# Two sweeps over d_ff and products from three float32r parts in an mLSTM cell with a feed-forward block

## The chip, the core and the metric

The kernel runs on one core of a Trainium2 chip. Its engines are TensorE (PE in the profile, with its weight loads shown apart as PEld), VectorE (DVE), ScalarE (ACT), GpSimd (POOL) and SyncE (SP), which here only issues DMAs. The metric is the device time of one execution in microseconds, median of several runs; smaller is better. All data are float32, apart from the weights, which lie in HBM as float64 and are read as 64-bit words (`U64`).

## The reference

An mLSTM cell runs over 4 batches, 8 heads, 768 tokens and head size 40; its output, 3072 tokens by 320, goes through a feed-forward block with d_ff = 2048:

```python
for t in range(S):                                   # per batch and head
    m_new = max(f_gate[t] + m, i_gate[t])
    C = exp(f_gate[t] + m - m_new) * C + exp(i_gate[t] - m_new) * outer(v[t], k[t])
    n = exp(f_gate[t] + m - m_new) * n + exp(i_gate[t] - m_new) * k[t]
    y[t] = sigmoid(o_gate[t]) * (C @ q[t]) / max(|n . q[t]|, 1)
x = y as (3072 tokens, 320)
h = x @ w_in                                         # 320 -> 2048
out = max(0.01 * h, h) @ w_out                       # 2048 -> 320
```

## The kernel before

**The cells.** The 768 tokens of a batch are cut into 6 chunks of 128; a step `s` is one chunk of one batch, with its 8 heads, and there are 24 steps, four to a chunk (`s = 4c + b`). Inside a chunk the recurrence is written as small matmuls with a decay mask: `u_parts` multiplies keys with queries (L598) and states with keys (L603), DVE applies the mask (L608) and adds to the state (L580), `u_mix` multiplies with the values and the state (L679), and DVE, POOL and DVE again turn that into x (L686, L617 to L619, L690, L693, L697). `gates` makes the decays of a chunk; they go to HBM (`a_dr`) and come back spread over the partitions (L397, L405).

**How a step's data comes.** Nearly all DMAs are issued by SP, in one order that the scheduler fixed when the program was built: k (L340), v in four pieces (L343), the decays (L397, L405), and k, q and the output gate in blocks, four DMAs each (L382). From chunk 2 on x goes out to HBM in four DMAs for a step (L700) and comes back transposed to `xT` in four more (L714). The steps use four rotating sets of buffers for k, v and the decays and two for the blocks (`rb`), so loads run two to four steps ahead.

**The weights** are loaded as 64-bit words (L213, L218) and made float32 by `narrow_weights`: one ACT and six DVE instructions per piece (L231 to L247). Both matrices are then held in SBUF whole.

**The feed-forward** runs per chunk, 512 tokens at a time (`ff_units`). First layer: the 320 inputs are cut in five slices of 64 rows; for each of the 16 blocks of 128 outputs five matmuls, 64 rows by 128 outputs by 512 tokens (for the first chunk 256), add up in PSUM. Two blocks go side by side, one on array rows 0 to 63, the other on rows 64 to 127 (`rows`, L743). ACT applies the leaky ReLU from PSUM to `acts` (L751). Second layer: for each of four groups of 128 tokens, 16 matmuls, 128 by 128 by 320 (`part`, L778), then an ACT copy and a DMA to the output (L786, L787). An f32 matmul appears in the trace as two weight loads and two matmuls, so L743 has 1120 instructions for 560 matmuls and L778 768 for 384.

**Order of the work.** PE, DVE, ACT and POOL run in the order in which the Python code emits it. `first_chunk` does chunk 0's cells. Then loop `c` = 1 to 6 emits the feed-forward of chunk c-1 as units (16 of first layer, 16 of second) and puts the cells of chunk c between them, at places written out by hand (`place`, `pairs`); in loop 6 there are no cells left. In loop 1 the remaining weights are narrowed, a few instructions per unit (`now`).

Of the kernel before, what the change touches and what calls it, by code (L numbers as in the profile page):

```python
# [9 lines left out]
F32 = mybir.dt.float32  # L10
U32 = mybir.dt.uint32
U64 = mybir.dt.uint64
AF = mybir.ActivationFunctionType
ALU = mybir.AluOpType
PSUM = bass.MemoryType.PSUM


@with_exitstack
def kernel(
# [51 lines left out]
    assert KR == DP and KC == 5 and KC * DP == Dm and GT * 4 <= 2048  # L71

    consts = ctx.enter_context(tc.tile_pool(name="consts", bufs=1))
    gp = ctx.enter_context(tc.tile_pool(name="gates", bufs=1))
    wk = ctx.enter_context(tc.tile_pool(name="wk", bufs=2))
    psf = ctx.enter_context(tc.tile_pool(name="psf", bufs=4, space=PSUM))
    psc = ctx.enter_context(tc.tile_pool(name="psc", bufs=4, space=PSUM))
# [22 lines left out]
    ident = consts.tile([P, P], F32, name="ident")  # L100
# [24 lines left out]
    acts = consts.tile([P, NF, GT], F32, name="acts")  # L125
    acts_l = acts[:].rearrange("p f t -> p (f t)")
    for n in range(NL):
        nc.vector.memset(kn[:, n, :, D:], 0.0)
        nc.vector.memset(qn[:, n, :, D:], 0.0)
        nc.gpsimd.memset(S_t[n][:, 1, :, D:], 2.0)  # L130
        nc.gpsimd.memset(S_t[n][SL:, 0], 0.0)
# [30 lines left out]
    QN = NF // 4  # L162
    QC = 4 * P
    WC = KC * 2 * P
    w_in = consts.tile([P, QN, WC], F32, name="w_in")
    w_out = consts.tile([P, NF, Dm], F32, name="w_out")

# [3 lines left out]

    def w_row(r, slot, j):
        n, e = divmod(j, 2)
        at = (2 * slot + e) * P
        return w_in[DP * r : DP * (r + 1), n, at : at + P]
# [6 lines left out]
    HW = 2 * Dm  # L182
    wide = moe_w_in.dtype == U64
    raws = {}
    if wide:
        raw_t = consts.tile([P, 5 * HW], U64, name="raw")

    def load_weights(n):

        m = n - QN  # L190
        if n < QN:
            dst = w_in[:, n, :]
        else:
            dst = w_out[:, 2 * m : 2 * m + 2, :].rearrange("p a d -> p (a d)")
        to = dst
        if wide:
            if n < 2:
                at = NF * GT - 2 * WC * (n + 1)
                raw = acts_l[:, at : at + 2 * WC].bitcast(U64)
            elif n < QN:  # L200
                raw = raw_t[:, WC * (n - 2) : WC * (n - 1)]
            elif m < 2:
                raw = w_out[:].rearrange("p f d -> p (f d)")[:, (2 + m) * WC : (3 + m) * WC].bitcast(U64)
            else:
                at = (4, 0, 1, 2, 3, 4)[m - 2] * HW
                raw = raw_t[:, at : at + HW]
            raws[n] = (raw, dst)
            to = raw
        if n < QN:
            src = moe_w_in[:, n * QC : (n + 1) * QC].rearrange("(k p) (r c) -> r p k c", p=DP, r=2)  # L210
            for slot in range(KC):
                for r in range(2):
                    nc.sync.dma_start(  # L213
                        to[DP * r : DP * (r + 1), 2 * P * slot : 2 * P * (slot + 1)], src[r, :, SLOTS[r][slot], :],
                    )
        else:
            rows = moe_w_out[2 * m * P : 2 * (m + 1) * P, :]
            nc.sync.dma_start(to.rearrange("p (a d) -> p a d", d=Dm), rows.rearrange("(a p) d -> p a d", p=P))  # L218

    def narrow_weights(n):  # L220
# [3 lines left out]
        if not wide:  # L224
            return
        raw, dst = raws.pop(n)
# [20 lines left out]
        nc.vector.tensor_tensor(dst, dst, low, op=ALU.add)  # L247


    a_dr = dr.tile([NB, 2, 2, BH, SL], F32, name="a_dr")  # L250
    x_dr = dr.tile([NS, Dm, P], F32, name="x_dr")
    gT, gL = {}, {}
# [95 lines left out]
    def load_o(s):  # L348
        c, b = divmod(s, B)
        at = NF * GT - 4 * WC - (s + 1) * Dm  # L350
        st[s]["o"] = acts_l[:, at : at + Dm]
        nc.sync.dma_start(  # L352
            st[s]["o"].rearrange("p (h d) -> p h d", d=D), o_gate[b, :, ts(c, P), :].rearrange("h p d -> p h d"),
        )
# [35 lines left out]
    def spread(s):  # L390
# [3 lines left out]
        w = wk.tile([P, H, P], F32, name="w", bufs=NL)  # L394
        d["w"] = w[:].rearrange("p h t -> p (h t)")[:, : H * SL].rearrange("p (h t) -> p h t", t=SL)
# [13 lines left out]
    def spread_first(a, s2):  # L409


        ab = [psf.tile([P, 2, H // RG, P], F32, name=f"ab{r}", tag="mm") for r in range(RG)]
        for n in range(2):
            for m in range(H // RG):
                for r in range(RG):
# [5 lines left out]
                    )  # L421
        for n in range(2):
            w = st[s2 + n]["w"] = wk.tile([P, H, P], F32, name="w", bufs=NL)
# [42 lines left out]
    def prep_qs(s):  # L466
# [3 lines left out]
        d["qs"] = wk.tile([P, Dm], F32, name="y")[:].rearrange("p (h d) -> p h d", d=D)  # L470
# [232 lines left out]
    def gather_x(s):  # L703

        c, b = divmod(s, B)
        if ("xT", c) not in st:
            st["xT", c] = wk.tile([P, KC, GT], F32, name="xT", bufs=1)
        xT = st["xT", c]
        src = x_dr[s].rearrange("(k p) t -> p k t", p=DP)
        for r in range(2):  # L710
            at = 0
            while at < KC:
                k0, n = run_of(r, at)
                nc.sync.dma_start(xT[DP * r : DP * (r + 1), at : at + n, ts(b, P)], src[:, k0 : k0 + 2 * n - 1 : 2, :])  # L714
                at += n

    def u_x(s):
# [3 lines left out]
        if b == 0:  # L721
            st["xT", c] = wk.tile([P, KC, GT], F32, name="xT", bufs=1)
        xT = st["xT", c]
# [9 lines left out]
        nc.scalar.copy(xT[DP:, 2 * KF, tok], xt[:DP, KF, :])  # L733
        del st[s]


    def ff_units(g):
        xT = st["xT", g]

        def rows(j, ph, cols, slots):  # L740
            for slot in slots:
                for r in range(2):
                    nc.tensor.matmul(  # L743
                        ph[r][:, cols], lhsT=w_row(r, slot, j), rhs=xT[DP * r : DP * (r + 1), slot, cols],
                        start=(slot == 0), stop=(slot == KC - 1),
                    )

        def relu(j, ph, cols):
            for r in range(2):
                f = f_of(r, j)  # L750
                nc.scalar.activation(acts[:, f, cols], ph[r][:, cols], AF.Prelu, alpha=0.01)  # L751

        def pair(j):
            ph = []

            def first():
                ph.extend(psf.tile([P, GT], F32, name=f"ph{r}", tag="mm") for r in range(2))
                rows(j, ph, slice(0, GT), range(3))

            def second():  # L760
                rows(j, ph, slice(0, GT), range(3, KC))
                relu(j, ph, slice(0, GT))

            return [first, second]

        def half(j, h):
            ph = [psf.tile([P, GT], F32, name=f"ph{r}", tag="mm") for r in range(2)]
            cols = ts(h, GT // 2)
            rows(j, ph, cols, range(KC))
            relu(j, ph, cols)  # L770
# [3 lines left out]
        def part(n, m):  # L774
            if m == 0:
                po[n] = psf.tile([P, Dm], F32, name="po", tag="mm")
# [254 lines left out]
```

## Time and profile before

| what | us |
|---|---|
| median of the runs (3; 527.35 to 528.73) | 528.12 |
| span of the profiled execution, first to last instruction | 526.4 |
| PE, PEld busy | 513.2, 336.3 |
| DVE, ACT, POOL busy | 240.3, 168.1, 113.0 |
| L743 and L778, matmuls of the feed-forward, busy on PE | 215.2 and 211.1 |

The profile has no other time for the profiled execution than its span; the median of the timed runs is 1.7 us above it. The page gives busy time of each engine, then the span in 40 equal slices of 13.2 us, then the chain of work that ended last and the costliest groups. In a group's row stand line, engine, operation, tiles (out<-in), shapes, count, then busy time and the mean of one in ns, then the engine's idle time before them. Matmuls overlap, so their busy time is less than count times mean. SP is in none of the busy rows: issuing a DMA is shown only in SP's own timeline (`SPq`), where each row is one stretch of issues, with its start and length.

The stages, by start and end on PE: chunk 0's cells to about 50 us, loop 1 to 139.6, loops 2, 3 and 4 to 218.5, 297.2 and 376.0, loop 5 to 454.0, loop 6 to the end.

### The profile page before, as it was taken

The page shows a single profiled execution, that of the slowest core. Times are in us where ns is not written, and L with a number is a line of the kernel's source. Part 1 is how long each engine was busy: PE and PEld are TensorE (multiplying, and loading weights), DVE is VectorE, ACT ScalarE, POOL GpSimd, SP SyncE. Part 2 cuts the span into 40 slices and gives each one's busy share as a digit, 9 for nine tenths or more (in the row PEclk, how much of TensorE's full clock was granted, in tenths as well). Part 3 has the DMA queues.
Part 4 walks back from the last instruction along what each step waited for, and adds up shares of the span by engine and source line. Part 5 has one row for each costly group of instructions (what it writes and reads, how often), then busy time and mean ns, then how long its engine had stood idle before and what let it go on. Part 6 is the DMA issues. An engine that isn't in the chain of part 4 may idle for free.

```text
span 526.4 us, 11333 instructions
## 1 busy us (share of the span) xinstructions
PE 513.2 (97%) x4501; PEld 336.3 (64%) x4501; DVE 240.3 (46%) x431; ACT 168.1 (32%) x458; POOL 113.0 (21%) x145
## 2 busy tenths in 40 slices
PE   8889989999999999999999999999999999999997
PEld 7877878777555577555577555577554577544675
DVE  4679998999328446028445028344028230000000
ACT  4565865534534212034212124212125100122100
POOL 4244354152205121015021015021013010000000
PEclk9668999999999999999999999999999999999999
DMA  9977687888755626685626676626542112000000
GB/s 116 156 204 153 138 212 171 196 145 175 146 137 105 137 72 150 129 174 107 138 75 143 134 150 129 138 76 155 125 102 52 50 52 87 14 0 1 12 12 25
DMA packets 165284, 59.13 MB, mean 112 GB/s; under 512 B 128816, under 2 KB 156016, under 8 KB 165232
## 3 DMA queue, kind: packets, MB, share of 16 engines
q1 hardware_dynamic: 164848, 58.28, 51.0%
q8 instruction: 35, 0.57, 0.5%
q10 hardware_dynamic: 384, 0.13, 0.1%
q14 instruction: 17, 0.14, 0.1%
HBM read 51.68 MB, written 6.70 MB: 111 GB/s over the span
## 4 chain that ended last, share of the span: by engine, by line
PE 83%; SPq 6%; DVE 4%; DMA 2%; ACT 2%; issue 1%; POOL 1%; ACTq 0%; POOLq 0%
PE po L778 38%; PE ph L743 36%; PE pT L679 3%; SPq L213 3%; PE sd L598 3%; SPq L338 2%; SPq L352 1%; PE sd L603 1%; DMA rb<-in_q_dram 1%; DVE raw L245 1%; DVE qn L608 1%; DMA S<-in_v_dram 0%; DMA raw<-in_moe_w_in_dram 0%; PE tk L518 0%; PE hN L649 0%
## 5 line engine op out<-in xcount | busy, mean ns | idle before, releaser
L743 PE MATMUL ph<-xT,w_in 64*128 64x512 f32 (+1 forms) x1120 | 215.2, 536 | 0.6 <-ACT acts L751 0.6
L778 PE MATMUL po<-w_out,acts 128*128 128x320 f32 x768 | 211.1, 434 | 0.0
L778 PEld LDWEIGHTS po<-w_out,acts 128*128 128x128 f32 x768 | 144.5, 190 | 62.6 <-issue 4.1
L743 PEld LDWEIGHTS ph<-xT,w_in 64*128 64x128 f32 x1120 | 107.8, 189 | 94.4 <-issue 87.7
L751 ACT ACTIVATE acts<-ph 128x512 f32<-128x512 f32 (+1 forms) x112 | 53.9, 534 | 151.8 <-PE ph L743 151.7
L608 DVE TENSOR_TENSOR qn<-w,sd 64x512 f32<-64x512 f32 x40 | 27.4, 684 | 97.7 <-PE sd L603 57.1
L576 POOL TENSOR_TENSOR S<-S,f 40x336 f32<-40x336 f32 x36 | 30.9, 858 | 101.9 <-PE pT L679 65.8
L442 ACT ACTIVATE w<-w,gT 128x64 f32<-128x64 f32 (+1 forms) x192 | 51.1, 348 | 3.1 <-POOL w L434 2.1
L434 POOL TENSOR_TENSOR w<-w,i 128x512 f32<-128x512 f32 x20 | 28.1, 1411 | 104.7 <-ACT bu L294 53.0
L786 ACT COPY y<-po 128x320 f32<-128x320 f32 x12 | 5.1, 423 | 83.3 <-PE po L778 83.3
L786 ACT COPY hn<-po 128x320 f32<-128x320 f32 x12 | 5.1, 426 | 76.0 <-PE po L778 76.0
L686 DVE STREAM_TRANSPOSE hb<-pT 128x512 f32<-128x512 f32 x16 | 11.4, 714 | 39.2 <-PE pT L679 39.0
L495 DVE TENSOR_TENSOR qn<-kqT,ea 64x512 f32<-64x512 f32 x32 | 27.3, 854 | 0.9
L693 POOL TENSOR_TENSOR xb<-xb,den 128x320 f32<-128x320 f32 x16 | 11.7, 728 | 66.5 <-DVE xb L690 66.5
L598 PEld LDWEIGHTS sd<-kqT 40*64 40x64 f32 x640 | 19.9, 135 | 6.1 <-issue 6.1
L697 DVE STREAM_TRANSPOSE x<-xb 128x512 f32<-128x512 f32 x16 | 18.1, 1130 | 7.7 <-POOL xb L693 7.7
L598 PE MATMUL sd<-kqT 40*64 40x64 f32 x640 | 21.5, 220 | 0.0
L603 PE MATMUL sd<-S,vu 64*40 64x42 f32 x576 | 20.1, 214 | 0.7 <-POOL vu L462 0.7
L489 DVE STREAM_TRANSPOSE kqT<-rb 128x512 f32<-128x512 f32 x32 | 20.5, 677 | 0.0
L603 PEld LDWEIGHTS sd<-S,vu 64*40 64x40 f32 x576 | 18.6, 111 | 0.8 <-POOL vu L462 0.8
L580 DVE TENSOR_TENSOR S<-S,sd 40x336 f32<-40x336 f32 x36 | 18.1, 503 | 1.0
L679 PEld LDWEIGHTS pT<-qn,S 128*64 128x64 f32 x512 | 15.6, 138 | 3.6 <-issue 3.5
(126 smaller groups left out, 364.9 us busy)
## 6 DMA issues: line engine op xcount, KB each, us to landing
w<-a_dr SPq DMA_DIRECT2D x40, 128.0 KB
rb<-in_k_dram SPq DMA_DIRECT2D x64, 80.0 KB
rb<-in_q_dram SPq DMA_DIRECT2D x64, 80.0 KB
rb<-in_o_gate_dram SPq DMA_DIRECT2D x64, 80.0 KB
ea<-a_dr SPq DMA_DIRECT2D x32, 128.0 KB
kn<-in_k_dram SPq DMA_DIRECT2D x24, 160.0 KB
raw<-in_moe_w_out_dram SPq DMA_DIRECT2D x6, 640.0 KB
S<-in_v_dram SPq DMA_DIRECT2D x80, 40.0 KB
```

The source lines that it names most:

```text
L434: nc.gpsimd.tensor_tensor(w, w, cm2.unsqueeze(1).to_broadcast([P, H, SL]), op=ALU.add)
L442: yield nc.scalar.activation(w[:, h, :], w[:, h, :], AF.Exp, bias=gT[c][:, 0, bh : bh + 1], scale=1.0)
L489: nc.vector.transpose(d["kqT"][:, i].rearrange("p (h t n) -> p h n t", n=TS, t=QW), raw_blocks(s, i, QW).rearrange("p (h n) d -> p h n d", ...
L495: nc.vector.tensor_tensor(mixed(s)[rows, 1 - r], d["kqT"][rows, 1].rearrange("p (h t) -> p h t", t=SL), d["ea"][rows], op=ALU.mult,)
L576: nc.gpsimd.tensor_tensor(new, old, g, op=ALU.mult)
L598: nc.tensor.matmul(bank[1 - u][toks, h, :], lhsT=kqT[rows, 0, ts(h, SL)], rhs=kqT[rows, 1, ts(h, SL)], start=True, stop=True,)
L603: nc.tensor.matmul(dC[u][:, h].rearrange("p k d -> p (k d)"), lhsT=d["ku"][toks, h], rhs=S_v[s % NL][toks, u, h, :, :V1], start=True, stop ...
L608: nc.vector.tensor_tensor(mixed(s)[toks, u], w[toks], bank[1 - u][toks], op=ALU.mult)
L679: nc.tensor.matmul(pT[DP * r : DP * (r + 1), j * P + u * SL : j * P + (u + 1) * SL], lhsT=S[:, u, h, :], rhs=m[:, u, h, :], start=True, st ...
L743: nc.tensor.matmul(ph[r][:, cols], lhsT=w_row(r, slot, j), rhs=xT[DP * r : DP * (r + 1), slot, cols], start=(slot == 0), stop=(slot == KC ...
L751: nc.scalar.activation(acts[:, f, cols], ph[r][:, cols], AF.Prelu, alpha=0.01)
L778: nc.tensor.matmul(po[n][:], lhsT=acts[:, f, ts(n, P)], rhs=w_out[:, f, :], start=(f == 0), stop=(f == NF - 1),)
```

## The change

- **Two sweeps.** d_ff is cut in two halves. Sweep 1 is the old loop with half of the weights: per chunk 8 units of first layer and 8 of second, then the partial output goes to HBM (`y_dr`, L821). Sweep 2 comes after the last loop: 12 groups of 256 tokens, each with 4 units; x comes back from HBM (L745), the partial sum too (L1092), and the result is written (L1142). Because sweep 2 needs all x in HBM, the x of chunks 0 and 1, which earlier never left SBUF, are now written out too (`keep_x`, L757).
- **Three parts.** A float32 number is split into its high part and the rest: `h` is the number with the low 12 bits masked off; the parts are h, the rest (scaled by 4096 on the weight side), and a combination of both (`three`, `split_x`). Three float32r matmuls (L786) give two PSUM sums, from which one scaled addition makes the product (`joined`, L795 ACT and L796 DVE). Both layers of sweep 2 and the first of sweep 1 are done so; the second layer of sweep 1 (L815) stays f32. All float32r matmuls of the first layer have 256 columns, those of the second 320.
- **Splitting work.** x is split on DVE, ACT and POOL (L269 to L272), once per sweep; the weights of the first half's w_in in `first_chunk`, those of the second half in loop 6 and the first units of sweep 2 (`convert_b`: narrowing, then L240 to L248, for four pieces of 128 by 1280). In sweep 2 the activations are split too (`grow`: three DVE instructions and a POOL copy of 128 by 512 per unit, L1112 to L1115).
- **Memory.** The cells' buffers are closed before loop 6 and their room is taken by the second half's weights; sweep 1's buffers are closed before sweep 2. PSUM for the feed-forward goes from four banks of their own to two buffers of two banks.
- The places of the cells between the units are written anew (`place`, `pairs`), the exponentials are emitted four instead of three per unit. The matmuls of the cells, their DMAs and their buffers' numbers stay.

Counted on the built programs, SP issues 607 DMAs before the change and 755 after it; DVE has 433 and 720 instructions, ACT 468 and 592, POOL 150 and 241. The float32r matmuls are 1440 (sweep 1, first layer), 1440 (sweep 2, first layer) and 576 (sweep 2, second layer); 192 f32 matmuls of the second layer are left. The core of the diff:

```diff
+    def three(raw, w, parts, eng):
+        h = raw.bitcast(F32)[:, :WC]
+        nc.vector.tensor_scalar(h.bitcast(U32), w.bitcast(U32), scalar1=HIGH, scalar2=None, op0=ALU.bitwise_and)
+        yield
+        nc.scalar.copy(parts[0], h)
+        eng.tensor_tensor(w, w, h, op=ALU.subtract)
+        yield
+        yield
+        nc.scalar.activation(parts[1], w, AF.Copy, scale=SPLIT)
+        yield
+        eng.tensor_tensor(parts[2], parts[1].bitcast(F32), h, op=ALU.subtract)
+        yield
...
+    def split_x(x, h, parts, eng):
+        nc.vector.tensor_scalar(h.bitcast(U32), x.bitcast(U32), scalar1=HIGH, scalar2=None, op0=ALU.bitwise_and)
+        nc.scalar.copy(parts[0], h)
+        eng.tensor_tensor(parts[1], x, h, op=ALU.subtract)
+        nc.vector.scalar_tensor_tensor(parts[2], in0=h, scalar=JOIN, in1=x, op0=ALU.mult, op1=ALU.subtract)
...
+    def keep_x(s):
+        to = x_dr[s].rearrange("(k p) t -> p k t", p=DP)
+        at = 0
+        while at < KC:
+            k0, n = run_of(0, at)
+            nc.sync.dma_start(to[:, k0 : k0 + 2 * n - 1 : 2, :], xT[:DP, at : at + n, ts(s % B, P)])
+            at += n
...
+    def product(j, w, xs, cols):
+        q, e = divmod(j, 2)
+        ph = psf.tile([P, 2, 2, GH], F32, name="ph", tag="mm")
+        for v in range(3):
+            for slot in range(KC):
+                at = (2 * slot + e) * P
+                for r in range(2):
+                    rows = slice(DP * r, DP * (r + 1))
+                    nc.tensor.matmul(
+                        ph[:, r, v // 2, :], lhsT=w[v][rows, q, at : at + P], rhs=xs[v][rows, slot, cols],
+                        start=(slot == 0 and v != 1), stop=(slot == KC - 1 and v != 0),
+                    )
+        return ph
+
+    def joined(ph, pool, out):
+        e = pool.tile([P, 2, GH], F32, name="e", bufs=2)
+        nc.scalar.copy(e[:], ph[:, :, 1, :])
+        nc.vector.scalar_tensor_tensor(out, in0=ph[:, :, 0, :], scalar=JOIN, in1=e[:], op0=ALU.mult, op1=ALU.add)
...
+        def first(j, half):
+            cols = ts(half, GH)
+            ph = product(j, wi, late_tiles["xs"], cols)
+            f = f_of(0, j)
+            a = acts[:, f : f + 3 : 2, cols]
+            joined(ph, fp, a)
+            nc.scalar.activation(a, a, AF.Prelu, alpha=0.01)
...
-        place = (2, 5, 7, 10, 12, 15, 16, 18, 21, 22, 24, 26, 28)
+        place = (1, 2, 3, 5, 6, 7, 8, 9, 10, 11, 12, 13, 13)
-        pairs = (2, 2, 6, 6, 14, 14, 19, 19, 19)
+        pairs = (1, 1, 4, 4, 8, 8, 10, 10, 10)
...
+            if c == NB:
+                cell.close()
+                open_b()
+                raw_b(0)
+                raw_b(1)
+                now = convert_b()
...
+                elif c == NB:
+                    run(now, 2 + i % 2)
...
+                if c > 1 and i == 1:
+                    split_a(1)
                 ffs[i]()
...
+                if c < NB and i == n_ff - 1:
+                    split_a(0)
...
+        def grow(u):
+            a = pending.pop(u)
+            h = fb.tile([P, 2, GH], F32, name="ah")
+            g = grown[u] = fb.tile([P, 3, 2, GH], F32R, name="g", bufs=4)
+            nc.vector.tensor_scalar(h[:].bitcast(U32), a[:].bitcast(U32), scalar1=HIGH, scalar2=None, op0=ALU.bitwise_and)
+            nc.gpsimd.tensor_copy(g[:, 0], h[:])
+            nc.vector.tensor_tensor(g[:, 1], a[:], h[:], op=ALU.subtract)
+            nc.vector.scalar_tensor_tensor(g[:, 2], in0=h[:], scalar=JOIN, in1=a[:], op0=ALU.mult, op1=ALU.subtract)
...
+        def leave(u):
...
+            for r in range(2):
+                for n in range(HB):
+                    for v in range(3):
+                        nc.tensor.matmul(
+                            po[:, n, v // 2, :Dm], lhsT=g[:, v, r, ts(n, P)], rhs=b1["wo"][v][:, f_of(r, j), :],
+                            start=(j == 0 and r == 0 and v != 1), stop=(j == NU - 1 and r == 1 and v != 0),
+                        )
...
+        for u in range(NH * NU + LAG):
+            hg, j = divmod(u, NU)
+            run(now, 4)
+            if u < NH * NU:
+                enter(u)
+            if 0 < u <= NH * NU:
+                grow(u - 1)
+            if j == 1 and hg + 1 < NH:
+                split_b(hg + 1)
+                if hg + 2 < NH:
+                    load_x2(hg + 2)
+            if u >= LAG:
+                leave(u - LAG)
```

`enter(u)` is `product` with the second half's weights, `joined` and a leaky ReLU on ACT; at the end of a group `leave` joins the two sums (L1133, L1135), adds the partial sum of sweep 1 (L1139) and writes the result.

## Prediction

> **What bounds the kernel now.** I read the engines' busy times and slices first, then the table of stretches by stage, then SP's own timeline.
>
> ```profile
> PE 513.2 (97%) x4501; PEld 336.3 (64%) x4501; DVE 240.3 (46%) x431; ACT 168.1 (32%) x458; POOL 113.0 (21%) x145
> ...
> PE   8889989999999999999999999999999999999997
> ...
> DVE  4679998999328446028445028344028230000000
> ...
> PEclk9668999999999999999999999999999999999999
> ```
>
> PE is busy from end to end; DVE is crowded only in the first quarter. The low clock digits (0.6) are in the second and third slice. By stage (PE, PEld, DVE, ACT, POOL busy; clock, DMA share, GB/s):
>
> ```profile
> 50.00:139.60 89.60, 86.33 (x1197) 68.32 (x1196) 80.14 (x118) 54.12 (x147) 36.52 (x35) 1.00 0.81 173
> ...
> 218.50:297.20 78.70, 78.70 (x680) 47.70 (x680) 34.30 (x64) 20.29 (x60) 17.35 (x20) 1.00 0.58 128
> ```
>
> Loop 3 is 78.7 us of PE: 34.5 first layer (L743), 34.7 second (L778), both read in loop 6 where nothing else runs, and 9.5 cells. So PE bounds it. But one queue that the busy rows leave out is nearly as full. SP's timeline in loop 3 (start, length, line, tiles, count):
>
> ```profile
> 241.86 1.47 SPq L700 DMA_DIRECT2D x_dr<-x  x4
> 243.43 1.79 SPq L382 DMA_DIRECT2D rb<-in_k_dram  x4
> 245.32 1.88 SPq L382 DMA_DIRECT2D rb<-in_q_dram  x4
> 247.29 1.12 SPq L405 DMA_DIRECT2D ea<-a_dr  x2
> 248.51 1.66 SPq L700 DMA_DIRECT2D x_dr<-x  x4
> 250.27 1.79 SPq L382 DMA_DIRECT2D rb<-in_k_dram  x4
> ...
> 261.86 5.88 SPq L714 DMA_DIRECT2D xT<-x_dr  x8
> ```
>
> The stretches follow each other without a gap worth naming. Summed over loop 3: 122 issues take 62.7 us, short gaps between them 8, real waiting 8 of 78.7. Loops 2 and 4: 60.1 and 64.6 us. From 0 to 139.6 SP issues 125.1 us, with 11.6 of short gaps and 3.7 of waiting. So in the part of the kernel that has cells, SP is the second bound, a tenth behind PE. The length of an issue is its own, not the queue's pushing back:
>
> ```profile
> L343 SPq DMA_DIRECT2D S<-in_v_dram x80: 595/628/3100, 41.8 to 384.4; - x80
> ...
> L714 SPq DMA_DIRECT2D xT<-x_dr x64: 573/606/1321, 183.1 to 441.2; - x64
> ```
>
> Minimum and median lie together, and L714 costs 0.6 us at 441 us too, when DMAs are few.
>
> **PE in the change.** A float32r matmul is not in this trace. Each has a weight load of 128 columns; fifteen of these stand alone at full clock here:
>
> ```profile
> 44.83 1.75 PEld L625 LDWEIGHTS pa<-S,w 128*128 128x128 f32 x15 [0.33 <-issue]
> ```
>
> (1.75 - 0.19)/14 = 0.111 us apart: the lower end. The upper end is an f32 instruction of the same columns: L743 60 x 64x256 in 6.75 us is 0.225 a pair; L778 34.66 us/128 is 0.27. An f32 matmul of 320 columns is two instructions, 0.54 us. The change's own algebra says that a product of split numbers is four part products; if f32 makes those four in 0.54, one takes 0.135, and a 256-column pair 0.112. That is an assumption; it lies at the lower row, and I take it. The Trainium skill, FP8 and Floating Point Precision, TensorE Precision Notes, says that true FP32 takes four passes through the array, high and low half of either operand; no row here shows a single pass, and by a quarter of the row's 0.54 the sum would be the 633 below.
>
> Sweep 1 per chunk: 8 units x 15 pairs x 0.112 = 13.4; 32 f32 matmuls x 0.54 = 17.3; cells 9.5: 40 us of PE instead of 79. Sweep 2 per unit: 15 x 0.112 + 12 x 0.135 = 3.3 us, 48 units.
>
> **SP in the change.** No issue of the cells goes. Up to the end of loop 1, 20 w_in (L213, 0.67) and 4 w_out issues go, 16 stores of x (L757) come, priced as L714's mean 0.63; with gaps of 0.07 that is -6.6 us. So loop 1 can end no sooner than 133. DVE there falls from 80 to 46 us (of 55 us of narrowing rows 16 stay, joins 5 come), PE to about 50; both lie under SP. In chunk 0 the weight splitting adds 2 x 3.9 us to DVE and the x splits 5; DVE is 90% busy from 30 to 50 us, so loop 1 starts some 10 us later, which its shorter DVE work gives back.
>
> Loops 2 to 4 keep 116 to 123 issues: 60 to 65 + 8 = 68 to 73 us, against PE's 40 and DVE's 45 (34.3; + 8 joins x 0.68 as L548; + 2 x (0.82 mask as L243 + 1.55 as L245)). **The wait that takes PE's place is SP's queue.** SP waits too: the x stores (L735) stand in its order ahead of the next block loads and wait for `u_mix`; behind them wait the gather, and for it the x split, and for that the next chunk's masks. Following one x store to that of the next chunk by rows (stores and gather 10, landing 2.4, split 4, two `u_parts` with masks 8, four units 7, two `u_mix` with transposes 15, second half the same without gather 20) gives 67 us. Two near-equal limits, and a PE that idles (clock 0.52 at 88% busy from 20 to 30 us, 0.67 at 74% from 30 to 40): I take 75 a loop, bounds 65 and 82. Start of loop 5: 133 + 3 x 75 = 358 (before: 376).
>
> The Trainium skill speaks against this floor: DMA: Bandwidth & Descriptors, Issuing engines are not separate DMA queues, calls the sequencer's issue time usually small against the DMA. The rows above, 62.7 of 78.7 us, disagree; by the page the three loops would fall to DVE's 45 us and the sum below to about 543 (an estimate).
>
> **Loop 5 to sweep 2.** After the last load (issued about there): landing 2.4, masks and exponentials 8, `u_parts` 6, units 4, `u_mix` with its DVE and POOL steps (0.71 + 0.60 + 0.49 + 0.73 + 1.13, twice) 9, stores 2, landing 2.4, gather 5.6: 40 us. Only then does SP come to the second half's weights: 10 issues and landing 9 us, then four pieces one after another, since the narrowing buffer is single. Per piece: ACT 1.38 (L231), DVE 0.94 + 1.38 + 1.69 + 0.82 + 1.72 + 1.56 (L233 to L247), mask 0.82, POOL 1280 elements at L434's or L693's rate 3.3 (bounds 2.9, 3.8), ACT 1.38: 15, with hand-offs 16. 64 us. Loop 6's PE work (31 us) hides under this. The first `leave` waits for piece 3, the third for piece 4, so under the wait PE does only 5 `enter` and 2 `leave`: 12 us. Cost: 40 + 9 + 64 - 12 = 101.
>
> **Sweep 2.** DVE per unit: join 0.68, mask 0.45, subtraction 0.77 (L495: 0.70 to 0.85), combination 0.75 (L241, L245 scaled) = 2.65; per group two of 1280 and one of 640: 3.2. Together 3.45 a unit, above PE's 3.3: DVE, in order and waiting on ACT's copy each time, paces it: 48 x 3.45 = 166 (bounds 158 by PE, 185 with a late hand-off). Last join, addition, store: 6.
>
> **Sum.** 358 + 101 + 166 + 6 = 631 of span; with the 1.7 us by which the median stands over the span, **633 us**, 20% slower. PE saves 90 us of 426; the saving is spent because before, PE's work hid SP's queue, and now a stage bound by SP is followed by one without cells, in line.
>
> **Rivals.**
> - *SP is no floor* (faster). If an issue took less when asked for faster, chunk 0 would end at 60, loop 1 take 50, loops 2 to 4 DVE's 45: 245 instead of 358, and 520 in all. It decides if the 550 issues up to loop 5 average below 0.45 us, gaps included; the rows have 0.64, and minima near medians speak against it. For it: the blocks' L382 has a minimum of 0.32 against 0.45.
> - *float32r at the f32 instruction's pace* (or built as two instructions, so that the change doesn't do what it says). Sweep 2: 48 x (15 x 0.225 + 12 x 0.27) = 318 instead of 166; sweep 1 hides it (54 us of PE under 75): 785. Against: the algebra above.
> - *Sweep 2 paced by hand-offs*: PE waits for `grow` each unit (ACT copy 0.59, join, leaky ReLU, three DVE steps, POOL copy): 4.2 a unit, 202: 669. Inside the range.
>
> **Chances.** Forecast with its bounds (low: SP at its medians without waits 324, then 84, PE's 158 and 8: 574; high: loop 1 to 145, three loops of 82, then 115, 185 and 8: 699) 0.82, hand-offs included; f32 pace 0.08; SP no floor 0.06; between 530 and 574 0.03; about equal 0.01. Faster or slower counts from 0.3%, about what a measurement of this kernel can tell: faster 0.06, same 0.01, slower 0.93. The range is 574 to 700.
>
> **What would show it.** SP's timeline solid in loops 2 to 4 with x stores its only waits, about 70 us of issues per chunk; PE busy near 5 in 10 until loop 5 and below that before sweep 2; pairs of L786 0.11 apart, L1126 0.135; DVE over 90% busy in sweep 2. I am wrong if loops 2 to 4 take 50 us, if L786's pairs are 0.2 apart, or if the weights' splitting is done before loop 6 ends on PE.

## The result, and the profile after

The changed kernel takes **840.34 us** (median of 4; 838.55 to 841.65) against 528.00 (527.35 to 528.73) in the same comparison: 1.591 times as long, interval 1.588 to 1.595. The forecast, 633 us with a range up to 700, was right in the sign and far too low. The profiled execution took 838.55 us, with a span of 836.8.

The page of the changed kernel, busy times and slices (20.9 us each):

```profile
PE 549.1 (66%) x6453; PEld 473.4 (57%) x6453; DVE 502.1 (60%) x718; ACT 278.9 (33%) x582; POOL 301.1 (36%) x236
...
PE   8644757785805393276608575764688888888886
...
DVE  5756625666613854075705554646777777777776
...
PEclk9555778997957897586958896787899999999999
```

PE's row had 97% before; now no engine is near full. Inside the part with cells PE has two slices with a 0, and the clock digit of both is 5: PE stands still there. By stage (PE, PEld, DVE, ACT, POOL busy; clock, DMA share, GB/s), the end of a loop taken at the ACT copy of a chunk's fourth output:

```profile
0.00:162.90 162.90, 107.32 (x1427) 92.02 (x1427) 92.70 (x164) 76.14 (x178) 56.49 (x77) 0.73 0.58 111
...
258.60:348.00 89.40, 45.84 (x694) 37.75 (x694) 45.35 (x77) 23.21 (x63) 25.57 (x23) 0.79 0.49 113
...
596.20:833.00 236.80, 201.03 (x1925) 182.88 (x1924) 184.88 (x222) 76.05 (x115) 114.23 (x69) 0.92 0.19 55
```

Loop 3 has 46 us of PE work in 89.4 us, loop 1 ends at 163 instead of 140. SP's issues cost what they did, minimum and median together:

```profile
L377 SPq DMA_DIRECT2D S<-in_v_dram x80: 595/627/1737, 34.9 to 434.9; - x80
...
L745 SPq DMA_DIRECT2D xT<-x_dr x64: 574/607/1527, 214.3 to 499.5; - x64
```

In loop 2 SP is solid: 82.5 us of issues and 9.9 of short gaps (up to 0.5 us), 92 of 95.7. But summed over loop 3, it issues 61.6 us and has 7.8 of short gaps: 69 of 89.4, not solid. What stops it is seen between 225 and 268 us. SP's timeline (start, length, line, tiles, count):

```profile
229.80 1.64 SPq L735 DMA_DIRECT2D x_dr<-x  x4
...
236.92 5.16 SPq L745 DMA_DIRECT2D xT<-x_dr  x8
242.18 1.97 SPq L416 DMA_DIRECT2D rb<-in_o_gate_dram  x4
...
255.42 1.00 SPq L821 DMA_DIRECT2D y_dr<-y  x2
...
258.86 0.34 SPq L821 DMA_DIRECT2D y_dr<-y  x1
```

ACT's, with the idle time ahead of an instruction and what ended it in brackets:

```profile
258.41 0.43 ACT L820 COPY y<-po 128x320 f32<-128x320 f32 x1 [31.09 <-DMA y_dr<-y]
258.73 1.26 ACT L270 CAST xs<-xh 128x1280 fp32r<-128x1280 f32 x1
```

And PE's:

```profile
260.04 5.08 PE L786 MATMUL ph<-xs,wi 64*128 64x256 f32 x60 [31.93 <-ACT xs L270]
```

ACT copies a partial output into one of two `y` buffers. Both wait for their stores, and the stores stand in SP's order behind 25 us of x stores, gathers and loads for the next steps (229.80 to 255.42). Behind ACT's copy stands ACT's part of the split of x, and for that PE waits 31.93 us. Such a wait of ACT comes once at the end of each of loops 2 to 4 (31.1, 27.6 and 28.2 us).

Sweep 2 takes 20.45 us per group. One group of it on PE:

```profile
679.20 3.44 PE L1126 MATMUL so<-vo,g 128*128 128x320 f32 x12 [3.15 <-DVE yo L1135]
682.57 2.10 PE L786 MATMUL ph<-xv,vi 64*128 64x256 f32 x30
684.60 2.03 PE L1126 MATMUL so<-vo,g 128*128 128x320 f32 x12
686.55 2.03 PE L786 MATMUL ph<-xv,vi 64*128 64x256 f32 x30
688.51 2.02 PE L1126 MATMUL so<-vo,g 128*128 128x320 f32 x12
```

By the last three starts, 12 second-layer matmuls take 1.95 us (0.163 each, forecast 0.135) and 15 pairs 1.96 (0.131, forecast 0.112): 15.6 us per group. To that come a wait of 3.15 us, and 1.5 us because PE then runs at half the pace for 3.4 us (here the 12 matmuls behind the wait, 3.44 us). The sum is 20.3.

### The profile page after: what moved, and what is told of

Its sections match the earlier page's. It is cut to its first block, busy times and chain, and to the rows that moved or that the text cites. A ratio compares the mean times of both kernels' runs of the same rounds, so it can differ in the third digit from the quotient of the medians.

```text
span 836.8 us, 16214 instructions
## 1 busy us (share of the span) xinstructions
PE 549.1 (66%) x6453; PEld 473.4 (57%) x6453; DVE 502.1 (60%) x718; ACT 278.9 (33%) x582; POOL 301.1 (36%) x236
## 4 chain that ended last, share of the span: by engine, by line
PE 30%; DVE 26%; SPq 15%; issue 9%; ACT 7%; POOL 6%; DMA 5%; DVEq 0%; ACTq 0%; POOLq 0%
PE ph L786 13%; PE so L1126 10%; SPq L745 4%; PE po L815 4%; DVE xh L269 3%; SPq L197 2%; SPq L416 2%; DVE acts L796 2%; DVE qn L530 2%; SPq L377 2%; ACT e L795 2%; DVE kqT L524 2%; DVE qn L643 2%; DVE g L1115 2%; POOL xs L271 1%
## 5 line engine op out<-in xcount | busy, mean ns | idle before, releaser
L786 PE MATMUL ph<-xs,wi 64*128 64x256 f32 x1440 | 125.1, 340 | 190.7 <-ACT xs L270 116.5
L786 PEld LDWEIGHTS ph<-xs,wi 64*128 64x128 f32 x1440 | 116.4, 244 | 198.8 <-ACT xs L270 119.1
L1126 PE MATMUL so<-vo,g 128*128 128x320 f32 x576 | 113.1, 352 | 39.8 <-DVE yo L1135 31.9
L1126 PEld LDWEIGHTS so<-vo,g 128*128 128x128 f32 x576 | 98.7, 216 | 47.8 <-issue 33.9
L815 PE MATMUL po<-w_out,acts 128*128 128x320 f32 x384 | 117.3, 457 | 12.5 <-ACT y L820 11.7
L796 DVE SCALAR_TENSOR_TENSOR acts<-ph,e 128x512 f32<-128x512 f32 x48 | 33.0, 688 | 147.9 <-ACT e L795 147.8
L786 PE MATMUL ph<-xv,vi 64*128 64x256 f32 x1440 | 102.8, 293 | 11.8 <-ACT xv L270 10.2
L786 PEld LDWEIGHTS ph<-xv,vi 64*128 64x128 f32 x1440 | 93.1, 195 | 22.9 <-ACT xv L270 10.7
L815 PEld LDWEIGHTS po<-w_out,acts 128*128 128x128 f32 x384 | 73.8, 199 | 47.7 <-ACT y L820 17.1
L795 ACT COPY e<-ph 128x512 f32<-128x512 f32 x96 | 55.8, 582 | 126.1 <-PE ph L786 126.1
L1113 POOL CAST g<-ah 128x512 fp32r<-128x512 f32 x48 | 51.5, 1073 | 102.5 <-DVE ah L1112 102.5
L796 DVE SCALAR_TENSOR_TENSOR a<-ph,e 128x512 f32<-128x512 f32 x48 | 33.1, 689 | 47.7 <-ACT e L795 47.6
L1115 DVE SCALAR_TENSOR_TENSOR g<-ah,a 128x512 fp32r<-128x512 f32 x48 | 52.7, 1097 | 0.0
```

The source lines that it names most:

```text
L786: nc.tensor.matmul(ph[:, r, v // 2, :], lhsT=w[v][rows, q, at : at + P], rhs=xs[v][rows, slot, cols], start=(slot == 0 and v != 1), stop=( ...
L795: nc.scalar.copy(e[:], ph[:, :, 1, :])
L796: nc.vector.scalar_tensor_tensor(out, in0=ph[:, :, 0, :], scalar=JOIN, in1=e[:], op0=ALU.mult, op1=ALU.add)
L815: nc.tensor.matmul(p, lhsT=acts[:, f, ts(n, P)], rhs=late_tiles["w_out"][:, f, :], start=(f == 0), stop=(f == FA - 1),)
L1113: nc.gpsimd.tensor_copy(g[:, 0], h[:])
L1115: nc.vector.scalar_tensor_tensor(g[:, 2], in0=h[:], scalar=JOIN, in1=a[:], op0=ALU.mult, op1=ALU.subtract)
```

## The experiments

Each is compared with 838.55 us, the profiled execution of the changed kernel, or with the kernel named. Each was timed once; the four runs of the changed kernel lie 3.1 us apart, so the time alone does not tell smaller differences from none. "Group" is a group of sweep 2.

**1. Is SP's queue a floor?** (`b_half`: in the kernel before)

```diff
-            for slot in slots:
+            for slot in [x for x in slots if x in (0, KC - 1)]:
...
-            for f in range(m * NF // 4, (m + 1) * NF // 4):
+            for f in (m * NF // 4, (m + 1) * NF // 4 - 1):
```

> The kernel before with half of the feed-forward's matmuls: of the five slices of the first layer only the first and the last, of every four matmuls of the second layer the first and the last; PE has some 40 us per loop left, as many as the changed kernel has in sweep 1, all else is untouched. Theory A (the prediction's step: SP's issues are the next floor): loops 2 to 4 take 70 to 75 us instead of 78.7, the whole 430 to 470 us. Theory B (SP issues faster when nothing holds it back, so it is no floor): loops 2 to 4 take 45 to 55 us, the whole 350 to 390 us.

442.72 us. Loops 3 and 4 take 73.6 us each; the stage table, same columns:

```profile
261.50:335.10 73.60, 46.49 (x518) 29.53 (x518) 32.84 (x65) 20.34 (x61) 16.99 (x21) 0.81 0.63 137
```

PE has 46 us of work, DVE 33, and SP's timeline in the same stretch has 63.5 us of issues and 7.9 of gaps: 71.4 of 73.6, or 0.58 us for each of 123 issues. Loop 2 takes only 50.7 us, less than theory A gave it; 79 issues fall into it (117 in the kernel before) and fill, with gaps, 46 us. So a loop is as long as the issues that are left for it, and theory A holds for loops 3 and 4: with PE's work gone, SP is what is left.

**2. The same with v's loads on ACT's queue** (`b_half_vact`)

```diff
-                nc.sync.dma_start(
+                (nc.sync if s < 2 * B else nc.scalar).dma_start(
                     S_v[n][ts(u, SL), u, :, i, :DB],
```

> The kernel before with half of the feed-forward's matmuls (as in the run before it, 443 us, loops of 73.6 us with SP issuing 63.5 us and 7.9 us of short gaps), and the loads of v from chunk 2 on, 16 per loop, issued from ACT's queue instead of SP's. Theory S (SP's issue time is the floor): 16 issues at 0.6 us and their gaps go, loops of 61 to 64 us, the whole 405 to 420 us. Rival C (the chain of dependences from the x store of one chunk to the next, estimated at 67 us, is as near): loops of 67 to 72 us, the whole 425 to 440 us.

418.00 us, 24.7 less. Loops 3 and 4 take 68.1 and 64.9 us; the second:

```profile
255.30:320.20 64.90, 46.58 (x518) 31.55 (x518) 33.65 (x61) 20.18 (x61) 17.38 (x20) 0.84 0.70 152
```

SP is at some 65 and 59 us in them, gaps included. The whole lies in theory S's range; the loops lie above its 61 to 64, one of them in the rival's range. So SP's issues were the floor, and the last 3 to 6 us per loop are no longer SP's: something else, by the rival the chain of the cells, is near.

**3. The stores of `y` from ACT's queue** (`a_yact`)

```diff
-                nc.sync.dma_start(y_dr[g, n], y[:])
+                nc.scalar.dma_start(y_dr[g, n], y[:])
```

> The changed kernel with the stores of the partial output issued from ACT's queue, where the copy that fills the buffer stands, instead of SP's. Theory Y (ACT's copy of the third group waits for one of two buffers, whose store stands in SP's order behind some 30 us of loads for the next steps; the split of x, and with it the next chunk's products, wait behind that copy): loops 2 to 4 go from 85 to 92 us to the 70 to 75 us of SP's issues, the whole from 837 to 760 to 790 us. Rival S (SP's issue rate alone): 24 issues less on SP, 4 per loop at 0.5 us: 2 us per loop, 825 us or more. Rival D (the join on DVE and ACT in order, with two PSUM buffers for the products, paces sweep 1): no change within 10 us.

839.86 us: no change, as rival D has it. But the reason is another one. ACT's wait for `y` is gone, while the scheduler put SP's DMAs in a new order, in which SP itself stands 29.0 us in two waits at block loads (L416) that the records put down to the stores of `y`. One wait was traded for another, so this run doesn't decide about theory Y.

**4. Two more buffers for `y`** (`a_y4`; the stores stay on SP)

```diff
-                y = fp.tile([P, Dm], F32, name="y", tag="y", bufs=2)
+                if n < 2 or g in (0, NB - 1):
+                    y = fp.tile([P, Dm], F32, name="y", tag="y", bufs=2)[:]
+                else:
+                    y = wk.tile([P, H, D1], F32, name="hn")[:].rearrange("p h d -> p (h d)")[:, :Dm]
```

> The changed kernel with the third and fourth partial output of a chunk in two other buffers (those of the output rows of the cells, hn, free after chunk 1), for the chunks 1 to 4; the stores stay on SP. Theory Y (buffers): the holes of 31 us in loops 3 to 5 close, loops 70 to 78 us, the whole 775 to 805 us. Rival S (SP's issue rate): SP issues the same, 830 to 840 us.

809.92 us, 28.6 less; the holes of 31 us are gone. Loops 2 to 4 take 65.7, 82.2 and 79.3 us, 227 together (277 in the changed kernel; forecast 225):

```profile
162.30:228.00 65.70, 46.87 (x694) 38.45 (x694) 42.51 (x75) 29.36 (x85) 25.51 (x22) 0.90 0.57 127
228.00:310.20 82.20, 49.93 (x694) 40.91 (x694) 46.86 (x80) 23.54 (x63) 24.36 (x22) 0.79 0.58 127
```

Loop 5 gives 15 us back (77.8 against 62.7): in the holes SP had worked ahead. In the changed kernel 151 issues fall into loop 2 and 47 into loop 5, here 102 and 84. The buffers of theory Y are the cause of the holes; their net price, 29 us, is smaller than it said (775 to 805 us), and loops 3 and 4 stay 8 to 10 us above SP's 71 to 72.

**5. The split of x behind `leave`** (`a_split`)

```diff
-            if j == 1 and hg + 1 < NH:
-                split_b(hg + 1)
...
             if u >= LAG:
                 leave(u - LAG)
+            if j == 1 and hg + 1 < NH:
+                split_b(hg + 1)
```

> The changed kernel with the split of the next group's x in sweep 2 emitted behind leave instead of ahead of it, so that the copy and the join that empty the four PSUM banks of the second layer no longer stand behind the split on ACT and DVE. Theory L (that order costs PE a wait of 3 us per group, after which its clock is at half for another 3.4 us): a group takes 16 to 17.5 us instead of 20.45, the whole 795 to 805 us when sweep 1 is unchanged, at most 50 us saved. Rival (DVE, whose work collides with POOL's, sets the pace of sweep 2): a group stays above 19.5 us, the whole above 825 us.

854.75 us, slower; a group takes 21.5 to 22.7 us. Theory L falls. PE in one group:

```profile
681.02 2.01 PE L1126 MATMUL so<-vo,g 128*128 128x320 f32 x12 [0.41 <-DVE yo L1135]
...
688.69 3.58 PE L1126 MATMUL so<-vo,g 128*128 128x320 f32 x12 [3.70 <-POOL g L1113]
```

The wait for the join is down from 3.15 to 0.41 us, and a wait of 3.70 for the parts of an activation (L1113) has taken its place, since those now stand behind the split on DVE and POOL.

**6. Three units of slack** (`a_y4_lag3`, on 4): `LAG = 2` becomes `LAG = 3`.

> The kernel with four buffers for the partial output (810 us) and, in sweep 2, the second-layer matmuls of a unit three units behind its product instead of two. Theory G (the split of the next group's x, 4 us on POOL and 4 on DVE, delays the parts of one unit by more than the one unit of slack, so PE waits some 3 us per group and then runs 3.4 us at half clock; the price is that of the order, not of the work): a group takes 16 to 17 us instead of 20.45, the whole 760 to 775 us. Rival (DVE and POOL in collision have no more room, 16 of 20.4 us busy): a group above 19 us, the whole above 792 us.

810.58 us, a group 20.8: no gain, as the rival has it. The wait stands at the join (3.54 us before L1129, that kernel's line for L1126), which now stands on DVE behind `grow`.

**7. Sweep 1's subtraction on DVE** (`a_y4_xdve`, on 4): in `split_a`, `nc.gpsimd` becomes `nc.vector`.

> The kernel with four buffers for the partial output (810 us), and in sweep 1 the subtraction of the split of x (128 by 1280) on DVE instead of POOL. Theory P (POOL's 4.1 us stands in the chain from the last cells of a chunk to the first product of the next, twice a chunk; on DVE it is 1.5 us): 2 to 2.6 us less, up to twelve times, of which the two of chunk 0 and one of each loop lie in the chain: 15 to 25 us less, 785 to 795 us. Rival S (SP's order sets the loops): only chunk 0 gains, 5 us, 805 us.

796.12 us, 13.8 less, 1 us short of theory P's range. Loops 3 and 4 take 75.6 and 75.1 us: now 4 us above SP's 71. Chunk 0, where theory P saw two of the gains, ends loop 1 only 0.8 us earlier, so the theory holds for the loops alone.

**8. Chunk 0's weights behind the cells** (`a_y4_c0`, on 4)

```diff
-        for _ in w:
-            pass
         u_transpose(3)
         run(prep_exp(3))
         prep_vu(3)
+        for _ in w:
+            pass
```

> The kernel with four buffers for the partial output (810 us), and in chunk 0 the rest of the first weight piece's narrowing and splitting emitted behind the last transposes and exponentials of the cells instead of ahead of them. Theory O (ACT's copy of the split weights waits 10.8 us for DVE's narrowing, and the cells' copy that PE waits 9.3 us for stands behind it): chunk 0 gets 7 to 10 us shorter, the whole 800 to 803 us. Rival W (the narrowing itself is what the first product waits for): no change within 3 us, or some us slower.

808.20 us, 1.7 less; loop 1 ends 2.7 us earlier. That is rival W's "no change within 3 us": ACT's wait of 10.8 us cost little by itself.

**9. The second w_out piece later** (`a_raw`, on 7)

```diff
-                    run(now, 2)
+                    run(now, 0 if i in (4, 5) else 4 if i > 5 else 2)
...
             load_w_out(1, raw_t[:])
+            yield
             yield from w_out_a(1)
```

> The kernel of 796 us, and in loop 1 the first step of the second w_out piece emitted three units later, so that ACT does not stand at it (9.9 us in the trace of the changed kernel) while its load, queued on SP behind the cells' loads, is on its way. Theory R (that wait holds up the cells' exponentials and so loop 1): loop 1 ends 6 to 10 us earlier, the whole 786 to 790 us. Rival (SP's order and the chain of the cells set loop 1 anyway): within 3 us of 796.

789.60 us, 6.5 less, and loop 1 ends at 155.0 instead of 161.5. Theory R holds: 6.5 of loop 1's excess is ACT standing, in the changed kernel for 9.9 us up to 115.7, at a load that SP issues only at 107.5 and 108.9.

**10. The last weight piece first** (`a_conv`, on 7): `run(now, 100)` between `load_x2(0)` and `split_b(0)`.

> The kernel of 796 us, and the last piece of the second half's weights converted ahead of the first split of x in sweep 2 instead of between it and the units. Theory Q (DVE's steps for that piece stand behind the split, which waits for x, which SP loads only behind the last stores of the partial output: 8 to 11 us): 785 to 790 us. Rival (the piece waits for its own load or for POOL, or its DVE work only moves in front of the split): no change within 3 us.

792.32 us, 3.8 less: between the two; under half of the 8 to 11 us that theory Q gave to that order.

**11. Sweep 2 reordered** (`a_s2`, on 7)

```diff
-        LAG = 2
+        LAG = 3
...
-            split_x(xb2[hg][:], h[:], [v[:] for v in t], nc.gpsimd)
+            split_x(xb2[hg][:], h[:], [v[:] for v in t], nc.vector)
...
+            if u >= LAG:
+                leave(u - LAG)
             if 0 < u <= NH * NU:
                 grow(u - 1)
...
-            if u >= LAG:
-                leave(u - LAG)
```

> The kernel of 796 us (four buffers for the partial output, subtraction of sweep 1's split on DVE), and sweep 2 reordered: the second layer three units behind the product and emitted ahead of the unit's own splitting, and the subtraction of the split of x on DVE instead of POOL. Theory G (the 20.45 us of a group are 15.6 of PE, 0.4 for the join, and the rest waits for in-order DVE and POOL with the half clock that follows them): a group 16.2 to 17.2 us, DVE nearly full, the whole 748 to 760 us. Rival (DVE's work itself, 16 us without collisions, plus its waits for ACT's copies, takes 19 us or more whatever the order): above 778 us.

780.02 us, 16.1 less; groups of 18.3 and 19.4 us in turn, 18.8 on average: between the two theories. DVE is now busy 149 of 171 us. So about a third of the excess over 15.6 us was the order and the engine of the split. Of what is left PE still waits for the join, 2.09 us in one group and 2.46 in the next; the groups of 19.4 us are those in which the clock falls to half after the longer wait (in the last section).

**12. All of these, and v's loads on ACT's queue** (`a_all`)

> All edits that gained taken together (four buffers for the partial output, split's subtraction on DVE, sweep 2 reordered, last weight piece ahead of the first split, second w_out piece later, first weight piece behind the cells), and besides the loads of v from chunk 2 on issued from ACT's queue. Theory (the excess over the prediction lies in these separate places, and under them SP's issue time is still the floor of the loops with cells): 780 - 4 - 6.5 - 2.5 = 767 us without the loads of v, and loops 2 to 4 from 75 to 65 us with them: 735 to 750 us. Rival (with the other edits made, the chain of dependences of the cells, not SP, sets the loops): 760 to 770 us. By neither does it come near the kernel before.

761.92 us: in the rival's range. Loops 2 to 4 take 72.5 to 75.0 us although SP's issues and gaps are down to 51 to 61. So in the changed kernel something else is as near as SP's queue; that it is the chain of the cells, with joins in line, is inferred and no run takes that chain apart.

**13. Sweep 1 without the three parts** (`a_f32s1`, on 4; core of the edit)

```diff
-            ph = product(j, wi, late_tiles["xs"], cols)
...
+            for slot in range(KC):
+                at = (2 * slot + e) * P
+                for r in range(2):
+                    rows = slice(DP * r, DP * (r + 1))
+                    nc.tensor.matmul(
+                        ph[:, r, 0, :], lhsT=wi[0][rows, q, at : at + P], rhs=xT[rows, slot, cols],
+                        start=(slot == 0), stop=(slot == KC - 1),
+                    )
...
-            joined(ph, fp, a)
-            nc.scalar.activation(a, a, AF.Prelu, alpha=0.01)
+            nc.scalar.activation(acts[:, f : f + 3 : 2, cols], ph[:, :, 0, :], AF.Prelu, alpha=0.01)
```

> The kernel with four buffers for the partial output (810 us), and the first layer of sweep 1 in plain f32 again: no splitting of x and of the first half's w_in, no join, one f32 product per unit. Theory H (in sweep 1 PE is not the bound, and what the splitting puts between the engines in chunk 0 and in each loop is on the path): loop 1 ends 15 to 25 us earlier than 162 us, loops 2 to 4 go from 80 to SP's 72 to 76 us, the whole 765 to 785 us, though PE has 4 us more work per chunk. Rival (SP and the cells alone set chunk 0 and the loops): 800 to 815 us.

751.98 us, 57.9 less: more than theory H said. Loop 1 ends at 136.6:

```profile
0.00:136.60 136.60, 100.22 (x1349) 81.53 (x1351) 74.74 (x147) 63.76 (x164) 50.32 (x76) 0.83 0.69 129
...
272.30:348.50 76.20, 54.09 (x616) 41.33 (x614) 32.85 (x65) 16.45 (x53) 16.96 (x21) 0.85 0.60 133
```

In that loop SP issues 64.0 us and has 7.8 of gaps: 71.8 of 76.2.

**14. Neither sweep with the three parts** (`a_f32`, on 13): the same edit in `enter`; `split_b` and `grow` do nothing; `leave` has four f32 matmuls instead of twelve float32r ones; weights are only narrowed.

> The same with sweep 2 in plain f32 too: the two sweeps of the change without its three parts, no splitting at all. Theory F (three float32r passes cost PE nearly what one f32 product costs: a unit of sweep 2 takes 1.95 + 1.95 us in the changed kernel against 2.25 + 2.16 us by the f32 rows of the kernel before, so the splitting buys 0.5 us of PE per unit and costs more than that in waits): sweep 2 from 236 us to 48 times 4.4, 212 us, its weights ready some 20 us sooner, the whole 715 to 745 us. Rival (float32r is what keeps sweep 2 short): sweep 2 above 240 us, the whole above 780 us. What remains above the kernel before is then the price of two sweeps.

705.78 us, the fastest with two sweeps and below theory F's 715 to 745, though its unit takes longer than the 4.4 us that theory F gave it. Sweep 2 is bound by PE alone, without a wait (the stretch, then units by start):

```profile
477.00:702.00 225.00, 222.74 (x1322) 155.94 (x1318) 9.90 (x12) 28.54 (x48) 0.00 (x0) 1.00 0.22 64
```

```profile
643.55 2.43 PE L1109 MATMUL ph<-xf,vi 64*128 64x256 f32 x20
645.91 2.42 PE L1127 MATMUL so<-vo,a 128*128 128x320 f32 x8
648.26 2.43 PE L1109 MATMUL ph<-xf,vi 64*128 64x256 f32 x20
```

An f32 unit takes 4.71 us (2.36 + 2.35), a float32r unit 3.91 (1.96 + 1.95). Three parts save PE 17%, and a group in f32, 18.8 us, is still shorter than the changed kernel's 20.45.

## Where the prediction was right and where wrong

The stages, in us, with the sum of the forecast beside four kernels. Sweep 2 starts, in this table, one group ahead of the end of its first; its column runs to the end of the span.

| kernel | loop 1 ends | loops 2 to 4 | to sweep 2 | sweep 2, tail | span |
|---|---|---|---|---|---|
| forecast | 133 | 225 | 101 | 172 | 631 |
| changed | 162.9 | 277.1 | 156.2 | 240.6 | 836.8 |
| 4: four `y` buffers | 162.3 | 227.2 | 176.6 | 242.0 | 808.1 |
| 13: and sweep 1 in f32 | 136.6 | 211.9 | 160.9 | 240.8 | 750.2 |
| 14: and sweep 2 in f32 | 136.6 | 209.9 | 132.1 | 225.4 | 704.0 |

Taken off in this order, the 310 us above the kernel before (526.4) are 29 for the two `y` buffers, 58 for the parts in sweep 1, 46 for those in sweep 2, and 178 for two sweeps as such.

- **"SP's queue takes PE's place": right as a floor.** Run 1 shows it in the kernel before, without the change: 71.4 of 73.6 us. Where buffers and splitting don't interfere (run 13), loop 1 ends at 136.6 (133 forecast) and loops 3 and 4 take 76 (75 forecast). The rival that SP is no floor, which needed less than 0.45 us an issue, is excluded by run 1's 0.58. SP is not the only limit at that height: run 12 takes some 10 us of issues per loop off it and the loops stay at 72 to 75. The 62.7 of 78.7 us that the forecast sets against a page are the sum of 122 issues; they do not contradict a sentence on one issue beside its own DMA (0.6 us here; a load of v landed after 2.37).
- **Loops 2 to 4, 75 us each: failed** at "x stores its only waits". I followed the x stores through SP's order, but not the stores of the new partial output, and did not ask which of ACT's and PE's work stands behind a full buffer. `y` and `hn` had been four buffers; the change keeps two. Measured: +52 us, of which four buffers take off 50 (run 4). That run 4 comes to 227, next to the forecast's 225, is partly luck: loop 2, with 102 issues, takes 66 us, and loops 3 and 4 take 82 and 79 because of the splitting (runs 7 and 13).
- **"Loop 1 starts some 10 us later, which its shorter DVE work gives back": failed.** Loop 1 ended 30 us late. I added the splitting's DVE time; but each split is a chain over DVE, ACT and POOL, with cells queued behind on the same engines. Run 13, without the parts, takes 26 of the 30 off. Which waits of the chain cost how much is settled only for 6.5 us (run 9) and some 3 (run 8).
- **101 us to sweep 2: failed** in three terms. "After the last load (issued about there)": in the changed kernel the last block load is issued at 469.9, 30 us after loop 5 starts, and the second half's weights start loading at 501.4, 61 us after it, not 40. In the kernel before it came as late (406.86, 31 us after), so this was a misreading of SP's order. Conversion lasted from 511.8 to 594.0, 82 us, not 64, with DVE and ACT also serving loop 6 and the first split in line. And the 12 us that PE was to do meanwhile don't show: three units' first-layer products were done (five were forecast), but the first `leave` came at 595.5. With loading (10 us, forecast 9) that is 21 + 1 + 18 + 12 = 52 of the 55 us.
- **Sweep 2, 3.45 us a unit, paced by DVE: failed.** A unit took 5.1. DVE was busy 79%, not over 90%. PE's own part was under-sized (3.91, not 3.3); DVE's steps came to 2.90 where they run alone, not 2.65. The larger part is PE's wait of 3.15 us for the join of a group's output (L1135), which stands on ACT and DVE behind the split of the next x, with the half clock after it: 4.65 us per group. The rival "hand-offs", 4.2 a unit, had such a wait, but at `grow` in every unit; at `grow` (L1113) PE waits only once between 600 and 800 us, for 0.7. Runs 5 and 6 show that this wait moves when the order is changed; run 11 gets a third of it back.
- **float32r: the mechanism right, the size off.** One instruction per matmul at about a quarter of f32's price: 0.131 for a pair and 0.163, forecast 0.112 and 0.135. The rival at f32's pace is excluded. What I missed is that three passes at a good quarter each leave only a sixth of PE's time to gain, in stages where PE isn't the bound. The 90 us of PE time that the forecast says are saved are 84 by its own terms (426 less 6 x 30.7 and 48 x 3.3).
- **Two sweeps cost 178 us** even without splitting. In run 14 loop 5 starts at 346.5, 30 us earlier than before (376); the rest of that kernel takes 357 us, against 150 before. What left the loops no longer fills the time under SP's issues, and comes back in sweep 2, where PE has 223 of 225 us. That the saving is spent in this way was in the forecast, and gave it its sign.

## What to carry to other kernels

Work that is moved out of a loop is gained only until the loop's next limit, here SP's issue time, and is paid in full where it lands. When a loop is shortened, list for each buffer that is reused which store frees it, in which queue that store stands, and what stands behind the instruction that waits; the number of buffers is a part of the change. Price a product in several parts with its splitting and joining as a chain through in-order engines, not as busy time per engine.

## What the runs showed of the hardware

**Half clock after a wait.** In sweep 2 of the changed kernel the granted clock (the seventh number of a stage row) falls to half for 3.4 us in nearly every group, after PE has waited for the join. In run 4 the wait is the same, 3.15 us, but the half clock comes at different places behind it (changed kernel, then run 4):

```profile
679.30:682.70 3.40, 3.40 (x14) 3.07 (x14) 3.37 (x3) 0.63 (x1) 3.40 (x3) 0.50 0.10 30
```

```profile
670.90:672.30 1.40, 1.40 (x10) 1.40 (x11) 1.40 (x2) 0.63 (x1) 1.40 (x2) 1.00 0.00 0
672.33:675.73 3.40, 3.40 (x28) 3.07 (x29) 3.22 (x3) 0.00 (x0) 2.70 (x2) 0.50 0.24 69
```

In the first the 12 matmuls behind the wait take 3.44 us instead of 2.0; in the second they take 2.36, and the 30 behind them 3.17 instead of 2.06. The price is about 1.5 us in both. How long PE must wait for it these runs do not fix: after a wait of 2.09 us in run 11 the clock stays full, after 2.10 us in run 12 it falls (run 11, then run 12):

```profile
671.29 2.00 PE L1129 MATMUL so<-vo,g 128*128 128x320 f32 x12 [2.09 <-DVE yo L1138]
```

```profile
557.07 3.41 PE L1130 MATMUL so<-vo,g 128*128 128x320 f32 x12 [2.10 <-DVE yo L1139]
```

In the kernels looked at, the clock stayed full after every wait of 0.41 us for the join, and fell after every one of 3.15 us or more. The Trainium skill, TensorE: Matmul & The Clock Gate, Part 1: The HAM clock gate, puts the fall to half clock at an idle window of about 3.4 us. The spells in these rows are as long as that window; but they follow waits that the profile shows as shorter, down to 2.1 us (the ends of matmuls are modelled).

**DVE and POOL stop each other.** In one group of the changed kernel, POOL first and then DVE:

```profile
676.45 4.16 POOL L271 TENSOR_TENSOR xv<-xf,xh 128x1280 fp32r<-128x1280 f32 x1 [1.42 <-DVE xh L269]
680.56 1.74 POOL L1139 TENSOR_TENSOR yo<-yo,yp 128x640 f32<-128x640 f32 x1
```

```profile
680.92 1.93 DVE L1114 TENSOR_TENSOR g<-a,ah 128x512 fp32r<-128x512 f32 x1
...
686.44 0.69 DVE L1114 TENSOR_TENSOR g<-a,ah 128x512 fp32r<-128x512 f32 x1
```

The same DVE subtraction takes 0.69 us alone and 1.93 beside L1139: it ends 0.55 us after POOL does. In the other direction POOL's subtraction takes 4.16 us when DVE's L272 starts just ahead of it, and 2.9 in the weights' splitting (L243); I had priced it at 3.3. The Trainium skill, SBUF — State Buffer, Who interferes with whom, says that a DVE instruction with two SBUF inputs contends with a GpSimd instruction that reads SBUF, and that this contention is an exclusive lock; these rows fit it.
